# An attention whose opening is loaded through two queues, with the first head's rows ahead of the second's, fill-in products and new ranks

## The chip, the core and the metric

The kernel runs on one core of one Trainium2 chip. The metric is the device time of one execution in microseconds, as the median of several runs. A core has five instruction queues that matter here: TensorE (PE; its weight loads are listed as PEld), VectorE (DVE), ScalarE (ACT), GpSimd (POOL) and SyncE (SP), which only issues transfers (DMAs).

## The reference

The reference has two stages. The first is attention over 4 batches of 8 heads, with 768 rows of 64 numbers each. Queries and keys are each assigned to the nearest of 16 centroids, and a query sees only the keys of its own cluster:

```python
q_assign = np.argmax(np.einsum('bhsd,hcd->bhsc', q_n, c_n), axis=-1)
k_assign = np.argmax(np.einsum('bhsd,hcd->bhsc', k_n, c_n), axis=-1)
mask = q_assign[:, :, :, None] == k_assign[:, :, None, :]
scores = np.where(mask, scale * np.matmul(q, k.transpose(0, 1, 3, 2)), -1000000000.0)
attn = np.exp(scores - np.max(scores, axis=-1, keepdims=True))
attn = attn / (np.sum(attn, axis=-1, keepdims=True) + 1e-09)
x = np.matmul(attn, v)
```

The second stage is a mixture of experts on the 3072 x 512 result: gate weights that are balanced in eight rounds, and for each of 8 experts `h = relu(x @ w1[e])`, `out += P[:, e] * (h @ w2[e])`.

## The kernel before

**The units.** Heads are worked in pairs (two heads share the 128 partitions), and groups of four heads share the loads of v. For a pair the raw rows of q and k are transposed on PE (L636), copied (L646), and split in a high and a low part (`qH`, `kH` by a cast at L654 or L656, `qL`, `kL` by a subtraction at L658 on DVE or L660 on POOL), so that products keep f32 accuracy. `assign_pair` multiplies the transposed rows by the normed centroids (PE L685), transposes the result (L693) and finds for each row its cluster in a chain on DVE: maximum `mx` (L699), equality `ix` (L704 or L706), tie-breaking by the constants `rev` (L712), `mi` (L717), and a one-hot matrix (`tx` for the first pair at L723, `om` for later ones at L758). Transposed back (L732, L765), its rows go into `qX` and `kX` (for the first pair directly by ACT L746 and DVE L742; for later pairs over `ot`, L772, and DMAs). `place_pair` moves halves of `qH`, `kL` and so on to where the products want them, by DMAs (L790).

**The heads.** For each of 32 heads and 9 chunks of a 768 x 768 score matrix, PE makes masked maxima (`max_chunk`, L835) in one of two `max_ps` buffers and DVE reduces them (L839). `max_rows` turns the maxima into three rows of `qX` (a reduce at L858, ACT L860, POOL L862 and L863; for heads 0 and 1 PE L873 and ACT L878, for later heads PE L885, ACT L889 and DMAs L893, L903). Only then can `exp_chunk` make the scores (PE L923, L924) and ACT the exponentials `pe` (L930), which POOL sums (L945). `values` multiplies by v (PE L978, L986), and `norm` scales the result and makes the second stage's input. Parts of the second stage (weights read and scaled early, `scan_early` and others) fill gaps; the experts' products (L1356, L1540 to L1542, L1814) make up the rest of the time.

**The order.** Inside the attention the order of the instructions on each engine is fixed when the program is built. Each unit is a process that yields its next step as `(engine, cost)`, and the class `Planner` lists the steps by start time and rank. A rank is

```python
return n * NCH + c + KEYS[stage] - (KEYS["first"] if n == 0 and stage in FIRST else 0)
```

and among the steps that could start within `EARLY` (`PATIENCE` after the first 30 of the plan's own time units) of the first one on that engine, the lowest rank goes first. Where a step could run on one of two engines, `RELUCT` weighs the choice. The numbers in these tables have no direct meaning, they are picked. On the chip each engine then runs its list in order and waits where an operand is late.

**The opening before the change.** SP issues the centroids (L356), q and k of pair 0 (L554), v (L567), q of pair 1, the gate's weights `wg` (L224), and k of pair 1, in this order. PE transposes the normed centroids first (L377), then q and k.

## Time and profile before

| what | value |
|---|---|
| median of three runs | 2289.27 us (2289.05 to 2291.24) |
| the profiled execution | 2289.5 us, of which 2287.7 us are the profile's span |
| PE busy | 2257.7 us of the span, 99% |
| DVE, ACT, POOL busy | 1637.3, 1113.2 and 1145.9 us |

The span is the time from the first to the last instruction of the profile, and the 1.8 us beside it lie outside the profile. A busy share says only that an instruction of the engine was under way: PE busy for 99% of the span has 1% of it without any instruction, and where that 1% lies is what the rows below show.

### The profile page before, as it was taken

To read this page: it belongs to the slowest core of one execution; us is meant where nothing else is said; L and a number is where in the kernel's file an instruction comes from. 1 tells how busy PE (TensorE), PEld (TensorE's weight loads), DVE (VectorE), ACT (ScalarE), POOL (GpSimd) and SP (SyncE) were. 2 spreads that over 40 slices of the span, in tenths; PEclk is the share of its full clock that TensorE was granted. 3 is DMA by queue.
4 is the path that set the end of the run, shared out by engine and by line. 5 is a ranking of instruction groups with operands and counts; after the bars stand their busy time and mean duration, and the time that the engine had idled before them with its cause. 6 is when DMAs were issued, how large, how long until landed. Compare 5 with 4: busy or idle time off the path is not lost.

```text
span 2287.7 us, 39676 instructions
## 1 busy us (share of the span) xinstructions
PE 2257.7 (99%) x15491; PEld 1523.3 (67%) x15491; DVE 1637.3 (72%) x2691; ACT 1113.2 (49%) x2048; POOL 1145.9 (50%) x1009
## 2 busy tenths in 40 slices
PE   7999999999999999999999999999999999999998
PEld 4656665545555555567777777777777777777777
DVE  7767777648666776578888886776676666666667
ACT  5666676556666665344444443333434333333333
POOL 6676777865554555456566563333332323222233
PEclk9999999999999999999999999999999999999999
DMA  7556666446645643676666665544444554344433
GB/s 173 120 125 162 168 157 159 118 167 239 196 150 170 195 158 131 221 262 212 211 233 219 226 222 177 169 128 152 151 159 137 187 169 133 129 132 137 143 116 102
DMA packets 226828, 383.93 MB, mean 168 GB/s; under 512 B 73408, under 2 KB 154640, under 8 KB 226128
## 3 DMA queue, kind: packets, MB, share of 16 engines
q1 hardware_dynamic: 226208, 379.82, 52.6%
q8 instruction: 121, 1.98, 0.4%
q10 hardware_dynamic: 432, 1.57, 0.2%
q14 instruction: 67, 0.55, 0.1%
HBM read 272.22 MB, written 80.62 MB: 154 GB/s over the span
## 4 chain that ended last, share of the span: by engine, by line
PE 92%; DVE 3%; DMA 2%; ACT 1%; POOL 1%; issue 1%; SPq 0%; ACTq 0%; DVEq 0%; POOLq 0%
PE h_ps L1356 37%; PE pb L1814 12%; PE pc L1814 8%; PE pa L1814 8%; PE av_ps L978 5%; PE o_ps L1540 3%; PE o_ps L1542 3%; PE o_ps L1541 3%; PE max_ps L835 3%; PE exp_ps L923 3%; PE exp_ps L924 2%; PE misc_ps L636 1%; PE misc_ps L1020 1%; POOL psum L945 1%; DVE mrt L839 1%
## 5 line engine op out<-in xcount | busy, mean ns | idle before, releaser
L1356 PEld LDWEIGHTS <-wa 128*128 128x128 f16 x5376 | 525.7, 98 | 300.0 <-issue 2.1
L1814 PEld LDWEIGHTS <-ho 128*128 128x128 f16 x6048 | 591.4, 98 | 139.7 <-DVE ho L1708 2.5
L1356 PE MATMUL h_ps<-xsT,wa 128*128 128x384 f16 x3072 | 581.6, 326 | 0.3 <-DVE u L1370 0.2
L1699 POOL TENSOR_TENSOR B<-B,B 128x768 f32<-128x768 f32 x96 | 196.5, 2049 | 488.2 <-DVE ho L1708 468.0
L1356 PE MATMUL h_ps<-xsB,wa 128*128 128x384 f16 x2304 | 436.7, 326 | 0.3 <-ACT m L1379 0.3
L1708 DVE TENSOR_TENSOR ho<-B,ho 128x768 f16<-128x768 f32 x288 | 350.2, 1217 | 0.1
L1370 DVE SCALAR_TENSOR_TENSOR u<-h_ps,m 128x384 f32<-128x384 f32 x256 | 141.7, 554 | 271.1 <-PE h_ps L1356 267.0
L1854 ACT ACTIVATE B<-B 128x384 f32<-128x384 f32 x288 | 149.7, 520 | 378.8 <-DVE B L1370 375.4
L1814 PE MATMUL pb<-w2o,ho 128*128 128x256 f16 x2592 | 328.7, 273 | 0.4 <-DVE ho L1708 0.4
L1704 ACT CAST ho<-B 128x768 f16<-128x768 f32 x288 | 230.3, 825 | 11.2 <-POOL B L1699 7.8
L839 DVE TENSOR_REDUCE mrt<-max_ps 128x1 f32<-128x512 f32 (+1 forms) x288 | 190.5, 685 | 54.3 <-PE max_ps L835 52.7
L945 POOL TENSOR_TENSOR psum<-psum,pe 128x512 f32<-128x512 f32 x160 | 208.0, 1318 | 35.0 <-ACT pe L930 28.1
L1814 PE MATMUL pa<-w2o,ho 128*128 128x256 f16 x1728 | 219.2, 273 | 1.2 <-DVE ho L1708 1.2
L1814 PE MATMUL pc<-w2o,ho 128*128 128x256 f16 x1728 | 219.2, 273 | 0.2 <-DVE ho L1708 0.2
L1699 POOL TENSOR_TENSOR B<-B,T 128x768 f32<-128x768 f32 x48 | 94.6, 1973 | 230.0 <-DVE ho L1708 207.7
L930 ACT ACTIVATE pe<-exp_ps 128x512 f32<-128x512 f32 x288 | 166.9, 598 | 51.2 <-PE exp_ps L924 39.5
L1379 ACT ACTIVATE m<-h_ps 128x384 f32<-128x384 f32 x128 | 62.6, 489 | 191.0 <-PE h_ps L1356 187.2
L1852 ACT ACTIVATE B<-h_ps 128x384 f32<-128x384 f32 x96 | 47.1, 490 | 203.3 <-PE h_ps L1356 203.3
L1542 PE MATMUL o_ps<-wb,hl 128*128 128x512 f16 x384 | 145.5, 379 | 0.0
L1541 PE MATMUL o_ps<-wb,hh 128*128 128x512 f16 x384 | 145.5, 379 | 0.0
L1540 PE MATMUL o_ps<-wb,hh 128*128 128x512 f16 x384 | 145.5, 379 | 0.0
L1370 DVE SCALAR_TENSOR_TENSOR B<-h_ps,u 128x384 f32<-128x384 f32 x192 | 105.9, 552 | 48.3 <-PE h_ps L1356 48.2
(266 smaller groups left out, 3320.8 us busy)
## 6 DMA issues: line engine op xcount, KB each, us to landing
wa<-w1d SPq DMA_DIRECT2D x98, 896.0 KB
w2o<-w2d SPq DMA_DIRECT2D x168, 512.0 KB
raw<-in_moe_w SPq DMA_DIRECT2D x64, 512.0 KB
w1d<-wa SPq DMA_DIRECT2D x30, 896.0 KB
r<-in_moe_w SPq DMA_DIRECT2D x28, 512.0 KB
w2d<-w2s SPq DMA_DIRECT2D x28, 512.0 KB
w2d<-wb SPq DMA_DIRECT2D x96, 128.0 KB
scan<-in_moe_w SPq DMA_DIRECT2D x32, 256.0 KB
```

Of the source, the lines that this page charges most:

```text
L839: nc.vector.tensor_reduce(out=t["mr"][:, i0 : i0 + ni, ni - 1], in_=ps.rearrange("p (x c) -> p x c", x=ni), axis=AX, op=ALU.max)
L930: nc.scalar.activation(pe, ps.rearrange("p (x c) -> p x c", x=ni), AF.Exp, scale=SCALE)
L945: (nc.gpsimd if e == POOL else nc.vector).tensor_tensor(out=st[:, o : o + N0], in0=old[o], in1=part, op=ALU.add)
L1356: nc.tensor.matmul(ps[:, 0:HB], wa[:, w_, a, c, :], x[:, x_, c, :], start=(first and s_ == 0), stop=(s_ == len(steps) - 1), skip_group_che ...
L1370: nc.vector.scalar_tensor_tensor(out=t, in0=ps[:, 0:HB], scalar=KAPPA, in1=x, op0=ALU.mult, op1=ALU.add)
L1540: nc.tensor.matmul(po[i], hh[:, t, ti], wbh[:, t], start=(first and t == 0), stop=False)
L1541: nc.tensor.matmul(po[i], hh[:, t, ti], wbl[:, t], start=False, stop=False)
L1542: nc.tensor.matmul(po[i], hl[:, t, ti], wbh[:, t], start=False, stop=(last and t == 1))
L1699: nc.gpsimd.tensor_tensor(out=t, in0=d[a], in1=d[c], op=ALU.subtract)
L1704: nc.scalar.copy(t[:, 0], blocks[n, g][o])
L1708: nc.vector.tensor_tensor(out=t[:, 1], in0=blocks[n, g][o], in1=t[:, 0], op=ALU.subtract)
L1814: nc.tensor.matmul(ps[:, q], h[:, h_, f, q * P : (q + 1) * P], w[:, 2 * g + f, w_], start=(first and g == 0 and s_ == 0 and q % 2 == 0), s ...
```

## The change

The change touches the opening of the attention, and some things that go on through all heads.

- **Two queues.** `load_first` issues q of pair 0 on SP as the first transfer of all, with the centroids behind it, and k on ACT's queue. The norm of the centroids (`csq`, `cnorm`, `cs`) becomes part of the process `centroid_rows` and is planned. The gate's weights are loaded behind the rows of head 1 (`gate_weights`), and some small constants are made later or no longer.
- **First head ahead of the second.** `assign_first` runs the DVE chain of pair 0 in two halves, head 0 first. `first_rows` transposes each head's q and k columns apart: 24 transposes of 32 x 128 in place of 6 of 128 x 128. `split_first` separates raw copy, high part and low part into steps with their own ranks.
- **Maxima in two parts.** `first_max` makes head 0's rows for its first four row tiles once chunks 0 to 5 are reduced, and those of the last two after chunk 8. The exponentials of head 0 go in the order `ORDER0`.
- **Products of constants.** `fill` issues bf16 products 128 x 384 of the constant `rev` into an `av_ps` buffer that nothing reads: 7 ahead of everything, and others where the planner sees PE idle in the first 36 of its time units. There are 41.
- **Fewer transfers.** From head 2 on, the two maxima rows go into `qX` in one DMA instead of two, and the two flag rows into `nht` in one (`mm` gets a fourth block for it).
- **Ranks.** `KEYS`, `EARLY`, `PATIENCE` and `RELUCT` get other numbers; loads of weights count as landed 1.5 later (`SLACK`). Over the program ACT makes all high parts (18 casts of DVE go to ACT), and 12 of DVE's subtractions go to POOL.

The diff, cut to its core:

```diff
--- before.py
+++ after.py
-    EARLY = {'PE': 0.171, 'ACT': 0.241, 'DVE': 0.196}
-    PATIENCE = {'PE': 0.009, 'ACT': 0, 'POOL': 0.384, 'SP': 0.102, 'DVE': 0.013}
+    FILLED = 36.0
+    EARLY = {'PE': 0.05, 'ACT': 0.01, 'DVE': 0.27, 'POOL': 0.06}
+    PATIENCE = {'PE': 0, 'ACT': 0.05, 'POOL': 0.69, 'SP': 0.06, 'DVE': 0.0}
...
+            if engine == "PE" and start < self.FILLED:
+                self.fill(int((start - self.free["PE"] - 0.2) * (3.0 if start < 10.0 else 4.5)))
...
-    nc.sync.dma_start(out=wg[:, :, 0:E], in_=w_gate.rearrange("(c p) e -> p c e", p=P))
...
-        nc.sync.dma_start(out=cn, in_=centroids.rearrange("h c d -> (h c) d"))
...
+            yield ev["load", 0, "k", "begun"]
+            yield ACT, 1.5
+            nc.scalar.activation(begun, ones[:, 0:1], AF.Sqrt)
+            yield ev["cn"]
+            yield DVE, 0.45
+            nc.vector.tensor_tensor(out=csq, in0=cn, in1=cn, op=ALU.mult)
+            nc.vector.tensor_reduce(out=cnorm, in_=csq, axis=AX, op=ALU.add)
+            yield ACT, 0.2
+            nc.scalar.activation(root, cnorm, AF.Sqrt)
+            yield DVE, 0.6
+            nc.vector.tensor_scalar(out=cnorm, in0=root, scalar1=1e-6, scalar2=None, op0=ALU.add)
+            nc.vector.reciprocal(cnorm, cnorm)
+            for x in range(2):
+                nc.vector.tensor_scalar(out=cs[:, x, :], in0=cn, scalar1=cnorm, scalar2=None, op0=ALU.mult)
...
+        def gate_weights():
+            yield ev["rows", 1]
+            yield SP, 3.1
+            nc.sync.dma_start(out=wg[:, :, 0:E], in_=w_gate.rearrange("(c p) e -> p c e", p=P))
+            plan.copied(0.3)
...
-        mm = [sm.tile([P, 3 * NT], F32R, name=f"mm{i}", bufs=1) for i in range(3)]
+        mm = [sm.tile([P, 4 * NT], F32R, name=f"mm{i}", bufs=1) for i in range(3)]
...
+        filler = rev.rearrange("p t c g -> p (t c g)")
+
+        def fill(n):
+            if n > 0:
+                ps = ps_v.tile([P, 1024], F32, name="av_ps")
+                for _ in range(n):
+                    nc.tensor.matmul(ps[:, 0:384], filler[:, 0:P], filler, start=True, stop=True)
+
+        plan.fill = fill
+        fill(7)
+        plan.free.update({PE: 4.0, ACT: 0.7, DVE: 3.0, POOL: 3.0, SP: 0.7})
...
-        KEYS = dict(load=-86.738, split0=-192.873, split1=-34.701, split2=-32.207, assign=-24.965, place=-68.504, chain=-64.418, ones=-184.712, max=-12.015, rows=-187.596, exp=8.794, values=49.904, out=19.77, batch=-51.141, group=-31.02, vsum=-10.101, group0=-186.961, inputs=-298.614, first=1197.688)
...
+        KEYS = dict(load=-49.03, split0=-481.28, split1=-156.05, split2=-168.62, assign=-129.16, place=418.41, chain=-633.91, ones=120.85, max=54.78, rows=-75.5, exp=67.53, values=104.0, out=44.0, batch=91.92, group=-108.42, vsum=45.1, group0=-435.34, inputs=-608.95, first=1434.49, high=23.78, low=-357.87, chain1=-806.64, ones1=-49.74)
...
-        RELUCT = [6.752, 2.462, 2.782, 2.846, 0.115, 0.25, -0.214, 1.339, -1.014, -0.069, 0.985]
-
...
+            if p == 0:
+                for w in (("q", q, nc.sync, SP, 4.9), ("k", k, nc.scalar, ACT, 5.1)):
+                    plan.spawn(load_first(*w), plan.now.key)
+                return
...
+            yield SP, 1.62
...
+        def load_first(name, src, by, engine, landed):
+            yield engine, 0.76 if name == "k" else 1.2
+            a = pairs[0][name] = nat.tile([P, NT, 2, D], F32, name=f"{name}n")
+            by.dma_start(out=a, in_=src[0, 0:2].rearrange("h (p t) d -> p t h d", t=NT))
+            if name == "q":
+                nc.sync.dma_start(out=cn, in_=centroids.rearrange("h c d -> (h c) d"))
+                ev["cn"].set(plan, 4.0)
+            plan.queues = landed - 0.95
+            ev["load", 0, name].set(plan, landed)
+            ev["load", 0, name, "begun"].set(plan)
...
+                if p == 1:
+                    if w == todo[-1][0]:
+                        t_x.put(plan)
+                    yield POOL, 0.2 + (z - a) * 0.0019
+                    nc.gpsimd.tensor_tensor(out=lo, in0=raw(p, w)[:, a:z], in1=hi.bitcast(F32), op=ALU.subtract)
...
+            N = 2 * NT
+            ix = nat.tile([P, N // 2, C, 4], BF16, name="ix", bufs=1).rearrange("p t c g -> p (t c g)").rearrange("p (x n c) -> p x n c", x=2, c=C)
+            mx, mi = (nat.tile(shape, dt, name=nm, bufs=1) for nm, shape, dt in (("mx", [P, 2 * N], F32), ("mi", [P, N // 2, 4], BF16)))
+            mi = mi.rearrange("p t g -> p (t g)")
+            om = om0[:, 0 : S // 2].bitcast(BF16).rearrange("p (x n c) -> p x n c", x=2, n=N)
+            for x in range(2):
+                plan.now.key = urgency("chain" if x == 0 else "chain1", 0)
+                sc = ps2[:, 0 : 2 * N * C].rearrange("p (n x c) -> p x n c", x=2, c=C)[:, x]
+                m, l, i_ = mx[:, x * N : (x + 1) * N], mi[:, x * N : (x + 1) * N], ix[:, x]
+                wide = lambda t: t.unsqueeze(2).broadcast_to([P, N, C])
+                yield DVE, 0.65
+                nc.vector.tensor_reduce(out=m, in_=sc, axis=AX, op=ALU.max)
+                nc.vector.tensor_tensor(out=i_, in0=sc, in1=wide(m), op=ALU.is_equal)
+                yield DVE2, 0.9
+                nc.vector.tensor_tensor(out=i_, in0=i_, in1=rev0.unsqueeze(1).broadcast_to([P, N, C]), op=ALU.mult)
+                nc.vector.tensor_reduce(out=l, in_=i_, axis=AX, op=ALU.max)
+                nc.vector.tensor_tensor(out=om[:, x, :, 0:C], in0=i_, in1=wide(l), op=ALU.is_equal)
+                if x:
+                    t_s.put(plan)
+                for j in (1, 0):
+                    plan.spawn(first_rows(om, x, j), urgency("ones" if x == 0 else "ones1", 0))
...
+        def first_rows(om, x, j):
+            yield t_m
+            yield PE, 0.25, 0.053, 0.06
+            psb = ps_m.tile([P, 512], F32, name="max_ps").bitcast(BF16)
+            for i in range(NT):
+                a = i % 2 * HS + i // 2 * P
+                nc.tensor.transpose(out=psb[0:Q, a : a + P], in_=om[:, x, 2 * i + j], identity=ident_b)
+            yield ev["clear", 0]
+            e = yield (ACT, 0.72), (DVE, 0.89)
+            o = buffers(0)[f"{'qk'[j]}X{x}"][64 : 64 + C, :]
+            if e == DVE:
+                nc.vector.tensor_scalar(out=o, in0=psb[0:C, 0:S], scalar1=(1.0, BIG)[j], scalar2=(0.0, -BIG)[j], op0=ALU.mult, op1=ALU.add)
+            elif j:
+                nc.scalar.activation(o, psb[0:C, 0:S], AF.Identity, scale=BIG, bias=om_neg[0:C, :])
+            else:
+                nc.scalar.copy(o, psb[0:C, 0:S])
+            t_m.put(plan)
+            ev["x", 0, x, "qk"[j]].set(plan)
...
+        def first_max(n):
+            m_ = mm[n]
+            mr = sm.tile([P, NT], F32, name="mr1")
+            for part, (i0, i1, c0, c1) in enumerate(((0, 4, 0, 6), (4, 6, 6, 9)) if n == 0 else ((0, NT, 0, NCH),)):
+                for c in range(c0, c1):
+                    yield ev["m", n, c]
+                t = heads[n]
+                k_ = i1 - i0
+                yield DVE, 0.09
+                nc.vector.tensor_reduce(out=mr[:, i0:i1], in_=t["mr"][:, i0:i1], axis=AX, op=ALU.max)
+                m3 = m_.rearrange("p (j t) -> p j t", j=4)[:, :, i0:i1]
+                yield ACT, 0.19
+                nc.scalar.copy(m3[:, 0], mr[:, i0:i1])
+                yield POOL, 0.59
+                nc.gpsimd.tensor_scalar(out=m3[:, 2], in0=mr[:, i0:i1], scalar1=-BIG / 2, scalar2=None, op0=ALU.is_le)
+                nc.gpsimd.tensor_tensor(out=m3[:, 1], in0=mr[:, i0:i1], in1=m3[:, 0].bitcast(F32), op=ALU.subtract)
+                if i1 == NT:
+                    plan.spawn(flag(n, mr), plan.now.key + 1)
+                if n:
+                    yield ev["rows", 0]
+                yield PE, 0.08 + 0.06 * k_, 0.107, 0.06
+                ps = ps_v.tile([P, 1024], F32, name="av_ps")
+                for i in range(i0, i1):
+                    nc.tensor.transpose(
+                        out=ps.bitcast(F32R)[0:3, i * P : (i + 1) * P], in_=m_.rearrange("p (j t) -> p t j", j=4)[:, i, 0:3], identity=ident_r
+                    )
+                for a, z in SPANS:
+                    if i0 * P <= a < i1 * P:
+                        yield ACT, 0.15 + (z - a) * 0.00083
+                        nc.scalar.copy(t["qa"][96:99, a:z], ps[0:3, a:z])
+                ev["half", n, part].set(plan)
+            ev["rows", n].set(plan)
...
-                yield SP, 1.5
-                for j in range(2):
-                    nc.sync.dma_start(
-                        out=qa[96 + j : 97 + j, :].bitcast(F32).rearrange("o (t p) -> o t p", p=P), in_=mt[j * NT : (j + 1) * NT, :]
-                    )
...
+            nc.sync.dma_start(out=qa[96:98, :].bitcast(F32).rearrange("o (t p) -> o t p", p=P), in_=mt[0 : 2 * NT, :])
...
-            for j in range(n % 2 * 2, n % 2 * 2 + 2):
-                nc.sync.dma_start(out=nh[j : j + 1, :].bitcast(F32).rearrange("o (t p) -> o t p", p=P), in_=flagged)
...
+            for r in (slice(j, j + 2),) if n > 1 else (slice(j, j + 1), slice(j + 1, j + 2)):
+                nc.sync.dma_start(out=nhs[n // 2 % 3][r, :].bitcast(F32).rearrange("o (t p) -> o t p", p=P), in_=flagged)
...
+        ORDER0 = (0, 1, 3, 4, 6, 7, 2, 5, 8)
...
-            yield ev["rows", n]
+            yield ev["half", 0, 0] if n == 0 and c % 3 < 2 else ev["rows", n]
...
-                yield ev["begun", n, c - 1]
+                yield ev["begun", n, ORDER0[ORDER0.index(c) - 1] if n == 0 else c - 1]
...
+        SLACK = 1.5
...
+                    yield plan.copied(1.1) - plan.now.time + SLACK```

**In the order, first place: PE from the start to the first chain.** `qn`, `kn` are the raw rows, `cs` the normed centroids, `cm` their transposed form, `rev` the constant of the fill-in products. Before:

```order
L377 MATMUL misc_ps<-ident,cs 128x128
L636 MATMUL misc_ps<-ident,qn 128x128 x4
L636 MATMUL misc_ps<-ident,kn 128x128 x4
L636 MATMUL misc_ps<-ident,qn 128x128 x2
L636 MATMUL misc_ps<-ident,kn 128x128 x2
L685 MATMUL exp_ps<-qn,cm 32x384
```

In the changed kernel, behind nine fill-in products (their repeats are left out in the middle):

```order
L677 MATMUL misc_ps<-ident,qn 128x128 x6
L677 MATMUL misc_ps<-ident,kn 128x128 x2
L677 MATMUL max_ps<-ident,kn 128x128 x4
L510 LDWEIGHTS rev
L510 MATMUL av_ps<-rev 128x384
...
L378 MATMUL misc_ps<-ident,cs 128x128
L717 MATMUL misc_ps<-ident,qn 128x128 x4
L764 MATMUL exp_ps<-qn,cm 32x384
```

The transposes of pair 0 now stand first, then ten products of constants (one is shown), and the centroids' transpose, which stood ahead of all, behind them; four transposes of pair 1 stand between it and the assignment.

**Second place: ACT, from the rows of head 1 on.** `pe` are exponentials, `ot` the one-hot rows of a later pair, `qX_200` and `qX_225` hold head 1's rows, and `spread` is a constant. Before:

```order
L878 CAST qX_225<-av_ps 3x512
L878 CAST qX_225<-av_ps 3x256
L646 COPY qn<-misc_ps 128x256
L646 COPY kn<-misc_ps 128x256
L930 ACTIVATE pe<-exp_ps 128x512
L646 COPY qn<-misc_ps 128x512
L930 ACTIVATE pe<-exp_ps 128x512
L654 CAST qH_205<-misc_ps 128x512
L930 ACTIVATE pe<-exp_ps 128x512 x2
```

In the changed kernel:

```order
L1037 CAST qX_200<-av_ps 3x512
L733 CAST qH_182<-misc_ps 128x256
L1037 CAST qX_200<-av_ps 3x256
L922 ACTIVATE ot<-misc_ps,om_bias,om_scale 64x384
L733 CAST kH_198<-misc_ps 128x256
L1115 ACTIVATE pe<-exp_ps 128x512
L486 CAST spread<-three_682 36x768
L1115 ACTIVATE pe<-exp_ps 128x512
L724 COPY qn<-misc_ps 128x512
L1115 ACTIVATE pe<-exp_ps 128x512
L733 CAST qH_180<-misc_ps 128x512
L1115 ACTIVATE pe<-exp_ps 128x512 x2
```

Copies and high parts of the next pairs stand among the exponentials in both. `ot` and `spread`, which stood ahead of head 0's exponentials before, now stand among them too.

**Third place: PE, where a pair's maxima begin.** The numbers are those of buffers; `kX_231` before and `kX_206` in the changed kernel are those of the head whose maxima begin. Before, with the semaphores that are waited for:

```order
L835 MATMUL max_ps<-kX_231,qX_227 128x512 [waits DMAHW6_49,DMAHW5_49,DVE_49]
L835 MATMUL max_ps<-kX_231,qX_227 128x512 [waits DVE_49]
L923 MATMUL exp_ps<-qL_218,kH_222 128x512 [waits Activation_49]
L924 MATMUL exp_ps<-qX_226,kX_230 128x512
L923 MATMUL exp_ps<-qH_205,kL_208 128x256 [waits Activation_49]
L924 MATMUL exp_ps<-qX_211,kX_214 128x256
```

In the changed kernel:

```order
L992 MATMUL max_ps<-kX_190,qX_187 128x512 [waits DVE_49] x2
L992 MATMUL max_ps<-kX_190,qX_187 128x256 [waits DVE_49]
L992 MATMUL max_ps<-kX_190,qX_187 128x256
L992 MATMUL max_ps<-kX_206,qX_202 128x512 [waits DMAHW4_49,DMAHW7_49,DMAHW2_49,DVE_49]
L992 MATMUL max_ps<-kX_206,qX_202 128x512 [waits DVE_49]
L992 MATMUL max_ps<-kX_206,qX_202 128x256 [waits DVE_49]
L992 MATMUL max_ps<-kX_206,qX_202 128x256
```

Where two maxima stood between exponentials' products before, six chunks of maxima in a row now stand there, and each needs one of the two buffers that DVE's reduces set free.

## Rows read from the trace of the kernel before

**Rows 1.** The page: the chain that ended last, shares of the span by engine.

```profile
PE 92%; DVE 3%; DMA 2%; ACT 1%; POOL 1%; issue 1%; SPq 0%; ACTq 0%; DVEq 0%; POOLq 0%
```

**Rows 2.** Windows: busy us of each engine (PE, PEld, DVE, ACT, POOL), PEclk, DMA.

```profile
0.00:32.00 32.00, 20.30 (x79) 11.27 (x79) 21.81 (x67) 14.08 (x28) 20.54 (x47) 0.96 0.64 155
32.00:51.70 19.70, 18.59 (x104) 14.27 (x102) 17.02 (x29) 15.21 (x31) 13.35 (x13) 0.89 0.74 180
51.70:100.00 48.30, 48.11 (x300) 28.25 (x300) 37.10 (x69) 27.58 (x64) 31.87 (x39) 1.00 0.58 133
```

**Rows 3.** Timeline: SP's issues and PE's first transposes (start, us, engine, line).

```profile
1.18 0.76 SPq L554 DMA_DIRECT2D qn<-in_q  x1
1.98 0.84 SPq L554 DMA_DIRECT2D kn<-in_k  x1
5.08 1.12 PE L636 MATMUL misc_ps<-ident,qn 128*128 128x128 f32 x4 [0.24 <-DMA qn<-in_q]
5.21 3.83 SPq L224 DMA_DIRECT2D wg<-in_moe_w_gate  x1
6.96 1.09 PE L636 MATMUL misc_ps<-ident,kn 128*128 128x128 f32 x4 [0.76 <-DMA kn<-in_k]
```

**Rows 4.** Timeline: the first pair's chain on DVE and its rows.

```profile
13.13 0.56 DVE L699 TENSOR_REDUCE mx<-exp_ps 128x24 f32<-128x384 f32 x1 [1.46 <-PE exp_ps L693]
15.29 0.79 DVE L723 TENSOR_TENSOR tx<-ix,mi 128x384 bf16<-128x384 bf16 x1
16.14 0.82 PE L732 MATMUL exp_ps<-ident_b,tx 128*128 128x128 bf16 x6 [0.91 <-DVE tx L723]
17.05 0.79 ACT L746 CAST qX<-exp_ps 16x768 fp32r<-16x768 bf16 x1 [1.20 <-PE exp_ps L732]
17.94 0.95 DVE L742 TENSOR_SCALAR kX<-exp_ps 16x768 fp32r<-16x768 bf16 x1 [1.26 <-ACT qX L746]
```

**Rows 5.** Timeline: DVE's first reduces, and the second pair's chain.

```profile
20.87 0.69 DVE L839 TENSOR_REDUCE mrt<-max_ps 128x1 f32<-128x512 f32 x1
25.55 3.30 DVE L839 TENSOR_REDUCE mrt<-max_ps 128x1 f32<-128x512 f32 x5
29.12 0.54 DVE L699 TENSOR_REDUCE mx<-misc_ps 128x24 f32<-128x384 f32 x1
31.27 0.36 DVE L758 TENSOR_TENSOR om<-ix,mi 128x384 bf16<-128x384 bf16 x1
```

**Rows 6.** Timeline: rows and first exponentials of heads 0 and 1, first values.

```profile
29.85 0.81 PE L873 MATMUL av_ps<-ident_r,mm 128*3 128x128 f32 x6 [0.44 <-POOL mm L863]
30.48 0.83 ACT L878 CAST qX<-av_ps 3x512 fp32r<-3x512 f32 x2 [0.32 <-PE av_ps L873]
31.94 0.78 PE L923 MATMUL exp_ps<-qH,kL 128*128 128x512 f32 x1
43.56 0.48 PE L923 MATMUL exp_ps<-qL,kH 128*128 128x512 f32 x1
51.70 2.58 PE L978 MATMUL av_ps<-pe,vn 128*64 128x512 f32 x14
```

**Rows 7.** Lines by form, 0 to 110 us: busy us, mean ns of one | idle before.

```profile
L654 ACT CAST kH<-misc_ps 128x512 fp32r<-128x512 f32 x5 | 3.0, 598 | 0.0
L930 ACT ACTIVATE pe<-exp_ps 128x512 f32<-128x512 f32 x50 | 29.0, 599 | 11.4 <-PE exp_ps L924 6.5 <-PE av_ps L978 2.0 <-PE misc_ps L885 2.0
L772 ACT ACTIVATE ot<-misc_ps,om_bias,om_scale 64x384 f32<-64x384 bf16 x8 | 5.3, 668 | 5.6 <-PE misc_ps L765 5.6
L472 ACT CAST spread<-three 36x768 bf16<-36x768 f32 x1 | 0.8, 826 | 0.0
```

**Rows 8.** Windows and timeline: PE at its two rates.

```profile
32.00:34.00 2.00, 2.00 (x8) 1.67 (x7) 1.54 (x3) 1.74 (x3) 0.00 (x0) 0.50 0.02 3
34.00:36.00 2.00, 2.00 (x8) 1.65 (x8) 1.66 (x4) 1.09 (x2) 0.81 (x1) 0.50 0.93 211
39.28 0.60 PE L636 MATMUL misc_ps<-ident,qn 128*128 128x128 f32 x4
```

289 lines of the change are left out of this document (173 added, 116 removed).

## The prediction

> **What bounds the kernel now.** I began with the chain that ended last [rows 1]. PE holds 92% of it, and DVE, DMA, ACT and POOL share what is left, so time can be won only where PE stands still or runs slowly. The windows say where that is [rows 2]. From 51.7 us on, PE is busy for 48.11 of 48.30 us: from the first product with v (51.70 [rows 6]) there is so much independent work that it hardly waits. Ahead of it PE is busy for 20.30 + 18.59 = 38.9 of 51.7 us. So 12.8 us are empty, and part of the rest is slow: in 32 to 36 us the granted clock is 0.50, the lower level of 1.2 GHz [rows 8], and four transposes that take 0.60 us at 39.28 [rows 8] take 1.12 at 5.08 [rows 3], though the clock column reads 1.00 there. The change works in these 52 us.
>
> Within them a chain across engines decides. In the timeline q is awaited until 5.08 and k until 6.96 [rows 3]; the chain of pair 0 runs on DVE from 13.13 to 16.08, and the rows go over ACT and DVE to 18.89 [rows 4]; DVE reduces head 0's maxima from 20.87 to 28.85 [rows 5]; the rows are done at 31.31, and the first scores start at 31.94 [rows 6]. For head 1 they start at 43.56, and the values at 51.70 [rows 6]. Were these three points all earlier by the same time, the kernel would be shorter by it.
>
> **The change part by part.** The sum is made against the profiled execution, 2289.5 us, which is 0.2 above the median.
>
> *Loads.* Before, q is issued at 1.18 and k at 1.98 [rows 3]. Now both start at about 0.7, so both end their issue near 1.5, where k ended it at 2.82 before. Bounds for the landing are 4.6 (q earlier by what it is issued earlier) and 7.0 (k as before); I take 5.4 for both, a third of the way, since k's issue is now where q's was. A rule speaks against this part. What the rows show: k is issued 0.80 us behind q, but its transposes start 1.88 us behind q's [rows 3]; something other than the issue spreads them. The Trainium skill, DMA: Bandwidth & Descriptors, Issuing engines are not separate DMA queues, says that transfers from several engines run on the same 16 DMA engines and interleave, and that only the issuing time is saved. By that, k gains about its issue and q loses what k takes of the bandwidth; by that alone k would land 1.3 earlier than before (the end of its issue, 2.82 to 1.5), at 5.7, and the sum would change by 0.3.
>
> *Centroids.* They land behind q now, and their norm, transpose and copies stand between q, k and the assignment on three engines. I count 2 us from q and k to the copies' end and 1.1 for the assignment, then `tr` and its transposes. From landed k to the chain took 6.2 us before (6.96 to 13.13), and I leave it 7.1: the chain starts near 12.5, 0.6 earlier. Bounds are 11.5 and 13.5: ten fill-in products stand ahead of the centroids' transpose on PE and could run on when it is ready.
>
> *Half a chain first.* The chain took 2.95 us for both heads [rows 4]. Half of its columns need less, but not half, since five operations start: I take 1.9, to 14.4. Then half of the transposes' 0.82 (I take 0.5), and `kX` and `qX` made side by side by ACT and DVE where they were made one behind the other (0.79, then 0.95 after a wait of 1.26 [rows 4]): head 0's maxima start near 16.1. The second half of the chain (1.07) then goes ahead of the first reduce, which I put at 17.1. It was at 20.87: **3.8 us** earlier. The 24 small transposes cost PE about 1 us more than six (18 x 0.06), in time that is empty.
>
> *Maxima in two parts.* Six reduces at 0.65 (five in 3.30 [rows 5]) end 4.0 behind the first. From the last reduce to the rows' end took 2.46 (28.85 to 31.31); with four tiles instead of six, half of the copies, and a few fill-in products I take 2.2. So head 0's first scores stand near 23.3, **8.6 us** earlier than 31.94. For head 1, 18 reduces (11.7) and the second pair's chain (31.63 - 29.12 = 2.5 [rows 5]) lie on DVE, then the rows (2.5), and about 1.6 for what else stands between: 18.3 behind the first reduce, near 35.4. That is **8.2 us** earlier than 43.56; the subtractions that went from DVE to POOL are in it.
>
> *From head 1's scores to the values.* Here the gain is at risk. In the order ACT has, between the first rows of head 1 and the next pairs' maxima, six full conversions at 0.60, five exponentials at 0.60, two `ot` at 0.67, `spread` at 0.83 [rows 7], the rows' copies of 0.83 [rows 6] and seven smaller ones, some 11.6 us. Before, `ot` and `spread` were behind it by then. DVE's subtractions and maxima wait for these casts. If all this stands in line, the values begin at 35 us behind the first reduce, 52.1, where they began at 51.70, and nothing is won. If the work that now comes earlier fills the time, the whole 8.2 is won, less 0.4 for work that PE has more of ahead of the values (four more transposes, one more vsum product, the 1 us of small transposes, two maxima fewer). I have no row that decides between these ends. I take half: **-4.1 us**.
>
> *Fill-in products.* They write a buffer that nobody reads, and stand where PE would be empty. At nothing, as long as the next operand is late; ten of them at the lower rate would hold the centroids' transpose for 1 to 2 us if it is ready early, which is in the bounds above. What they do to the clock is a rival.
>
> *Transfers, weights of the gate, SLACK.* 60 DMAs fewer leave SP's queue. All DMA waits together are 2% of the chain [rows 1], and no row says how much of it is theirs: bounds -3 and 0, and I take 0, for the rows of a later head have a head's time ahead of them. `wg` held SP for 3.83 us ahead of k of pair 1 [rows 3]; moved, it holds the moves of later pairs, at most 3.8 us for these alone, hidden behind the pair that is under way. SLACK delays early weights for which PE does not wait here: 0.
>
> *Casts and subtractions.* ACT takes 18 casts of DVE, about 8 us at 0.60 or less each [rows 7] over all heads. ACT is busy for 27.58 of 48.30 us [rows 2], so I cost it at nothing; without that cover it is at most 8.
>
> Sum: 2289.5 - 4.1 = **2285.4 us**.
>
> **The rivals.** *The clock stays up.* The granted clock fell before, after a stretch in which PE waited for DVE between maxima, and was 0.50 through 32 to 36 us [rows 8] in which PE had work all along. If the fill-in products hold it at 2.4 GHz, head 0's scores also run at twice the rate, some 2 to 4 us more, and nothing goes back: -8 to -13. For it: several of the products stand exactly ahead of head 0's scores, where the clock was low. Against it: they stand in gaps of a plan, and real gaps may lie elsewhere. The Trainium skill, TensorE: Matmul & The Clock Gate, Part 1, says that activity releases the throttle, which is for this rival; its Part 4 says that transposes do not count the same way, and most of the opening's early work is transposes. The trace agrees in so far as the first transposes ran at half rate [rows 3]. Chance 0.20.
>
> *The opening moves and the end does not.* The values start where they started, for the queue of ACT above, and what was done early only leaves other gaps: -2 to +3, chance 0.15.
>
> *Slower: maxima in bursts.* PE fills one of two `max_ps` buffers while DVE reduces the other, so two reduces (1.3 us) must pass between a chunk and the one after the next. Where PE has less other work between them in its list, it waits. By the durations of the rows, counted along the order, 9 such places lacked 2.3 us in all before, and 34 lack 13.7 now. If DVE is not ahead there, up to 11.4 us come back over all heads, and with part of the opening's gain kept the kernel is 4.6 to 10 slower. Against it: DVE is busy for 37.1 of 48.3 us [rows 2], and where PE comes late to a burst nothing is lost. It decides when more than some 8 of the 11.4 us are real. Chance 0.15.
>
> **How the numbers follow.** The likeliest case, part of the gain kept, has 0.50 and its own range from 2281.3 (all of 8.2) to 2290. A change of 0.2%, 4.6 us, is what a measurement of this kernel can tell from none. Of the 0.50, 0.24 lie below -4.6 and 0.26 above. Faster: 0.24 + 0.20 = 0.44. Same: 0.26 + 0.15 = 0.41. Slower: 0.15. For the range I go 11.5 down, which leaves out the far end of the clock's case, and 4.5 up, which leaves out most of the bursts': 2278 to 2294.
>
> **What would show it.** In the trace after: k's first transposes below 6; the first reduce near 17, head 0's first scores near 23 and head 1's near 35 (each right or wrong by itself); the values' first product between 43.5 and 52 (my sum says 47.6); the granted clock from 20 to 36 us (near 1 is the first rival's case); idle time of PE put down to `mrt` behind 52 us (over 8 us is the third's). The prediction is wrong if the values start as late as before, if the fill-in products turn the clock, or if the gain of the opening is paid back by waits for maxima.

## The result, and the profile after

The changed kernel takes 2307.67 us (median of six runs, 2306.82 to 2308.81) against 2288.91 us before: the ratio is 1.0082 with a 95% interval from 1.0069 to 1.0095. It is 18.8 us slower, where 2285.4 was forecast.

The first view is the windows of the changed kernel (columns as in [rows 2]).

```profile
0.00:52.00 52.00, 42.97 (x209) 26.70 (x210) 30.22 (x77) 27.25 (x55) 38.71 (x67) 0.85 0.66 146
52.00:66.00 14.00, 7.91 (x37) 4.58 (x37) 8.62 (x18) 3.86 (x10) 8.58 (x14) 0.74 0.71 170
66.00:110.00 44.00, 43.62 (x271) 24.88 (x270) 26.03 (x49) 23.55 (x54) 27.07 (x33) 0.98 0.36 82
```

PE is full from 66 us on, where it was full from 52 us on [rows 2]. The 42.97 us of the first row hold 11.8 us of fill-in products (the windows of L510 alone). Without them PE has been busy by 66 us for as long as it had been by 52 before (39.1 and 38.9 us).

The timeline of the changed kernel shows what came when (start, us, engine, line). L591 are the loads, L677 the transposes of q, L374 and L378 the centroids, L764 and L837 the assignments of the first and the second pair, L785 the start of the first chain, L996 DVE's reduces, L806 the transposed one-hot rows, L1108 scores, L992 maxima, L630 the sums of v, L1163 the values and L1545 the experts.

```profile
0.72 0.71 ACTq L591 DMA_DIRECT2D kn<-in_k  x1
0.72 0.77 SPq L591 DMA_DIRECT2D qn<-in_q  x1
7.31 1.51 PE L677 MATMUL misc_ps<-ident,qn 128*128 128x128 f32 x6 [2.05 <-DMA qn<-in_q]
11.12 1.17 DVE L374 TENSOR_SCALAR cs<-cn,cnorm 128x64 f32<-128x64 f32 x2
12.91 0.27 PE L378 MATMUL misc_ps<-ident,cs 128*128 128x128 f32 x1
13.73 0.51 PE L764 MATMUL exp_ps<-qn,cm 128*32 128x384 f32 x1
15.80 0.36 DVE L785 TENSOR_REDUCE mx<-exp_ps 128x12 f32<-128x192 f32 x1 [2.12 <-PE exp_ps L773]
21.02 2.56 DVE L996 TENSOR_REDUCE mrt<-max_ps 128x1 f32<-128x512 f32 x4
28.31 0.82 PE L806 MATMUL max_ps<-ident_b,tx 128*32 128x128 bf16 x6
30.16 0.88 PE L1108 MATMUL exp_ps<-qH,kL 128*128 128x512 f32 x1
31.40 0.85 PE L837 MATMUL misc_ps<-qn,cm 128*32 128x384 f32 x1
33.53 1.29 DVE L996 TENSOR_REDUCE mrt<-max_ps 128x1 f32<-128x512 f32 x2 [1.99 <-PE max_ps L992]
42.92 0.47 PE L1108 MATMUL exp_ps<-qL,kH 128*128 128x512 f32 x1
53.97 0.69 PE L992 MATMUL max_ps<-kX,qX 96*128 96x512 f32 x2
63.78 0.79 PE L630 MATMUL misc_ps<-vsum,ones 128*128 128x256 f32 x1 [4.66 <-POOL vsum L626]
65.78 3.54 PE L1163 MATMUL av_ps<-pe,vn 128*64 128x512 f32 x16
509.97 1.14 PE L1545 MATMUL h_ps<-xsB,wa 128*128 128x384 f16 x6
```

The kernel before has the second pair's assignment and the first product of the experts here:

```profile
22.34 0.85 PE L685 MATMUL misc_ps<-qn,cm 128*32 128x384 f32 x1
491.72 1.14 PE L1356 MATMUL h_ps<-xsB,wa 128*128 128x384 f16 x6
```

Read against [rows 3 to 6]: q's transposes start 2.2 us later than before, the first reduce at the same time (21.02 and 20.87), head 0's scores 1.8 us earlier, head 1's 0.6 us earlier, and the values 14.1 us later. The expert products begin at 509.97, before at 491.72: 18.2 us later, and what follows takes the same 1796 us. So the whole loss lies in the attention: 14.1 us by the first product with v, and some 4 us behind it.

For these 4 us one row stands out: PE's weight loads of the maxima from 75 us to the experts, by line, with the idle time ahead of them and what ended it. First the kernel before, then the changed one:

```profile
L835 PEld LDWEIGHTS max_ps<-kX,qX 96*128 96x128 f32 x327 | 56.2, 190 | 23.2 <-DVE mrt L839 7.6 <-DMA qX<-ot 2.8 <-issue 2.8
```

```profile
L992 PEld LDWEIGHTS max_ps<-kX,qX 96*128 96x128 f32 x342 | 59.2, 190 | 22.4 <-DVE mrt L996 12.5 <-issue 1.2 <-DMA kX<-ot 0.5
```

They waited 12.5 us for DVE's reduces, where they had waited 7.6. A weight load can wait while an earlier product still runs, so this is no measure of lost time by itself: between the first product with v and the experts PE is busy for 434.83 us in place of 430.20, with as many products (2680 and 2683), and without an instruction for 9.4 in place of 9.8 us. So the 4 us lie within PE's busy time, and the row alone doesn't show how many of them are the waits.

### The profile page after: what moved, and what is told of

Same layout as the page of the kernel before. It is cut to its first block, busy times and chain, and to the rows that moved or that the text cites. A ratio compares the mean times of both kernels' runs of the same rounds, so it can differ in the third digit from the quotient of the medians.

```text
span 2305.5 us, 39696 instructions
## 1 busy us (share of the span) xinstructions
PE 2273.9 (99%) x15550; PEld 1530.8 (66%) x15550; DVE 1626.2 (71%) x2676; ACT 1120.3 (49%) x2065; POOL 1156.8 (50%) x1021
## 4 chain that ended last, share of the span: by engine, by line
PE 92%; DVE 3%; POOL 1%; ACT 1%; issue 1%; DMA 0%; ACTq 0%; SPq 0%; DVEq 0%; POOLq 0%
PE h_ps L1545 37%; PE pb L2003 12%; PE pc L2003 8%; PE pa L2003 8%; PE av_ps L1163 5%; PE o_ps L1729 3%; PE o_ps L1730 3%; PE o_ps L1731 3%; PE exp_ps L1108 3%; PE max_ps L992 3%; PE exp_ps L1109 2%; DVE mrt L996 1%; PE misc_ps L1205 1%; PE misc_ps L717 1%; POOL psum L1130 1%
## 5 line engine op out<-in xcount | busy, mean ns | idle before, releaser
L1545 PEld LDWEIGHTS <-wa 128*128 128x128 f16 x5376 | 525.7, 98 | 299.6 <-issue 1.6
L1545 PE MATMUL h_ps<-xsT,wa 128*128 128x384 f16 x3072 | 581.6, 326 | 0.1
L1545 PE MATMUL h_ps<-xsB,wa 128*128 128x384 f16 x2304 | 436.7, 326 | 0.3 <-ACT m L1568 0.3
L996 DVE TENSOR_REDUCE mrt<-max_ps 128x1 f32<-128x512 f32 (+1 forms) x288 | 191.4, 686 | 68.1 <-PE max_ps L992 65.5
L1115 ACT ACTIVATE pe<-exp_ps 128x512 f32<-128x512 f32 x288 | 167.7, 600 | 53.9 <-PE exp_ps L1109 46.4
```

Source lines behind the costliest of these rows:

```text
L996: nc.vector.tensor_reduce(out=t["mr"][:, i0 : i0 + ni, ni - 1], in_=ps.rearrange("p (x c) -> p x c", x=ni), axis=AX, op=ALU.max)
L1115: nc.scalar.activation(pe, ps.rearrange("p (x c) -> p x c", x=ni), AF.Exp, scale=SCALE)
L1545: nc.tensor.matmul(ps[:, 0:HB], wa[:, w_, a, c, :], x[:, x_, c, :], start=(first and s_ == 0), stop=(s_ == len(steps) - 1), skip_group_che ...
```

## The experiments

Three theories on the opening stood first: **L**, two loads at once make q late; **F**, the fill-in products are in the way; **V**, the values wait in PE's list behind work that is late. The first four kernels tell them apart.

**e1, one queue.**

```diff
-                for w in (("q", q, nc.sync, SP, 4.9), ("k", k, nc.scalar, ACT, 5.1)):
+                for w in (("q", q, nc.sync, SP, 4.9), ("k", k, nc.sync, ACT, 5.1)):
```

> The changed kernel with k of pair 0 issued on SP behind q and the centroids; nothing else moves in any order. Theory L (the two loads share the DMA engines, so q lands at 7.3 us where it landed at 5.0 before, and the opening starts from there): q's first transpose near 5.5 instead of 7.3, the first reduce near 19.5 instead of 21.0, and the kernel 1 to 2 us faster than the changed one. Theory V (the time is lost in the order between head 1's scores and the first product with v): values still begin near 64 to 66 us, and the kernel is within 2 us of the changed one, near 2307.

2307.71 us, as the changed kernel. The timeline of e1 has q's transposes where L wants them:

```profile
5.33 1.17 PE L677 MATMUL misc_ps<-ident,qn 128*128 128x128 f32 x6
6.98 0.44 PE L677 MATMUL misc_ps<-ident,kn 128*128 128x128 f32 x2 [0.48 <-DMA kn<-in_k]
```

But the assignment starts at 13.17 (13.73 before the edit), since the centroids and the second pair's q stand ahead of it, the first reduce at 21.28, where L wanted 19.5, and the values at 65.69. L is right about q's landing, and by itself it changes nothing.

**e2, no fill-in products.**

```diff
-            if n > 0:
+            if n > 99:
                 ps = ps_v.tile([P, 1024], F32, name="av_ps")
```

> The changed kernel without its 41 products of constants (leaves out work that nothing reads). Theory F (the fill-in products hold up the centroids' transpose and heads' scores): the first reduce 1 to 2 us earlier and the kernel 1 to 3 us faster than the changed one. Rival (they keep the clock up and pay for themselves): the granted clock is lower between 12 and 24 us and the kernel 1 to 3 us slower. Theory V: within 1 us, values still near 65.

2309.56 us; the interval of its ratio to before, 1.0072 to 1.0099, overlaps that of the changed kernel. The first reduce starts at 20.82 and the values at 64.82, so F falls. Its rival is not settled: the granted clock from 12 to 24 us is 0.68 in place of 0.96, as the rival has it, but the 1.9 us of time can't be told from none.

**e3, the first group's sums ranked lower.**

```diff
-            plan.now.key = urgency("vsum", n)
+            plan.now.key = urgency("vsum", n) - (200.0 if n == 0 else 0.0)
```

> The changed kernel with the rank of the sums of v of the first group of heads lowered by 200, so that on PE their product (L630) stands ahead of head 1's scores' end and the first product with v stands ahead of the second group's. Theory V (the first product with v waits in PE's list behind the second group's product, for which POOL's ten additions were awaited for 4.7 us): values begin near 57 to 59 instead of 65.8, and the kernel is 6 to 9 us faster than the changed one, near 2300. Theory L or F: values' start moves but other waits take its place, and the kernel stays within 2 us of 2307.

2302.34 us, 5.3 less. The product of the sums and the first product with v in the timeline of e3:

```profile
49.53 1.05 PE L630 MATMUL misc_ps<-vsum,ones 128*128 128x256 f32 x2
54.84 1.51 PE L1163 MATMUL av_ps<-pe,vn 128*64 128x512 f32 x6
```

In the changed kernel these sums stood at 57.87, and the values behind the second group's product, for whose sums PE waited 4.66 us (63.78 in the timeline). Now the values start 11 us earlier, more than V had, and half of that reaches the end: 5.3 us, a little below its range.

**e4, the kernel before with k on ACT's queue.**

```diff
-                nc.sync.dma_start(out=a, in_=src[b, 2 * hp_ : 2 * hp_ + 2].rearrange("h (p t) d -> p t h d", t=NT))
+                (nc.scalar if p == 0 and name == "k" else nc.sync).dma_start(out=a, in_=src[b, 2 * hp_ : 2 * hp_ + 2].rearrange("h (p t) d -> p t h d", t=NT))
```

> The kernel before, with k of pair 0 issued on ACT's queue and nothing else changed. Theory L: q and k land together near 6.5 to 7, k's wait goes and q's comes, and the kernel is 0 to 2 us slower than before. My forecast's step (q and k both land near 5.4): the chain of pair 0 starts about 1 us earlier and the kernel is up to 1 us faster. Theory V: nothing that can be measured.

2290.07 us, ratio 1.0001 (0.9993 to 1.0010): nothing that can be told. In its timeline q's transposes start at 6.32 instead of 5.08 [rows 3] and the values at 52.49 instead of 51.70 [rows 6], the way L has it and against my forecast's step.

What was left was why the second pair is late: its assignment starts at 31.40 in the changed kernel, at 22.34 before. `assign_pair` takes a token that the first pair gives back. Now that the second head's rows come last, the first pair holds it until they are written. That is theory **P** (the pair); theory **C** is the centroids' chain.

**e5, centroids first**, their norm ahead of the planned steps, and all three loads on SP (e1's edit too).

```diff
+        nc.sync.dma_start(out=cn, in_=centroids.rearrange("h c d -> (h c) d"))
         csq = nat.tile([P, D], F32, name="csq", bufs=1)
...
+        nc.vector.tensor_tensor(out=csq, in0=cn, in1=cn, op=ALU.mult)
+        nc.vector.tensor_reduce(out=cnorm, in_=csq, axis=AX, op=ALU.add)
...
         def centroid_rows():
-            yield ev["cn"]
-            yield DVE, 0.45
-            nc.vector.tensor_tensor(out=csq, in0=cn, in1=cn, op=ALU.mult)
...
```

> The changed kernel with the centroids as the first transfer, their norm ahead of the planned steps and all on SP's queue, as before; its planner moves other steps a little. Theory C (the centroids' norm behind q's copies on DVE holds pair 0's assignment until 13.7 us): assignment near 10, first reduce near 17.5 to 18.5 instead of 21.0, head 0's scores near 26 to 27, kernel 2 to 4 us faster than the changed one. Theory P (the second pair comes too late, whose assignment starts at 31.4 instead of 22.3): head 2's maxima and the values stay near 50 to 64, and the kernel is less than 2 us faster.

2311.67 us, 4 us slower where C had 2 to 4 faster. The assignment starts at 9.67, head 0's scores at 25.47 and the values at 53.76, all as C has them or better. The re-planned order has more bursts of maxima, chunks of maxima in a row that wait for DVE (16.4 us in the row of the weight loads instead of 12.5). These 3.9 us are not enough for 12 us of lost gain. The windows of e5 show more:

```profile
75.00:85.00 10.00, 8.30 (x42) 5.09 (x41) 9.29 (x18) 6.20 (x15) 8.99 (x12) 0.98 0.56 128
85.00:95.00 10.00, 9.42 (x32) 5.47 (x31) 7.33 (x14) 2.43 (x7) 3.71 (x8) 0.50 0.40 95
95.00:105.00 10.00, 9.26 (x25) 6.36 (x26) 7.71 (x15) 3.56 (x8) 2.06 (x5) 0.50 0.60 132
```

The granted clock is 0.50 from 85 to 105 us, behind a run of maxima that waited for DVE; in the changed kernel it is 1.00 there.

**e6, the token given back when the chain is done.**

```diff
+            t_sc.put(plan)
             for w in "kq":
                 yield ev["x", 0, 1, w]
             ev["om", 0].set(plan)
-            t_sc.put(plan)
```

> The changed kernel with one line moved: the token that lets the next pair's assignment begin is given back when the first pair's chain is done, not when the second head's rows of the first pair are written. Theory P: the second pair's assignment starts near 21 to 23 instead of 31.4, its first maxima near 46 to 49 instead of 54.0, and the kernel is 4 to 8 us faster than the changed one. Theory V alone (group 0's sums): the first product with v is still behind POOL's sums, and the kernel is within 2 us of 2307.

2305.24 us. The second pair's assignment starts at 20.52 and its maxima at 43.64 instead of 53.97, as P says. The values still wait for the sums, until 61.10, and 2.4 us reach the end, where P had 4 to 8.

**e7, e3 and e6 together; e8, with e5 too.**

> Both: the token given back early and the rank of the first group's sums lowered by 200. If P and V are two causes that add: 9 to 13 us faster than the changed kernel, 2295 to 2298. If they are one (PE lacks work in the same time): 5 to 7 us, as the group's rank alone, near 2301.

> Centroids ahead on SP, the token given back early, and the first group's rank lowered. If C, P and V are the opening's whole loss: 13 to 18 us faster than the changed kernel, 2290 to 2294, and what is left above the kernel before is the bursts of maxima (about 4 us in the trace of the changed kernel). If the opening has another cause: above 2297.

e7 takes 2306.64 us, slower than either expectation, although its values start at 52.36; e8 takes 2293.98, with values at 46.05. So P and V together are shown to be 13.4 of the 14.1 us by which the values were late, and an early opening alone doesn't decide the time. Behind its values e7 needs 456.82 us up to the experts, the changed kernel 444.19; its row of weight loads says 15.6 us, and its granted clock is 0.77 in 105 to 120 us and 0.66 in 320 to 330. Theory **B**, the bursts, was left to test. By the order alone I counted the places where two chunks of maxima have less than 1.25 us of other PE work between them, and what they lack: 2.4 us before, 13.8 in the changed kernel, 18.0 in e7, 10.8 in e8 (the last two counted after these kernels had run). One rank changes it.

**e9 and e10, the changed kernel with the rank of the maxima 30 or 70.**

```diff
-        KEYS = dict(... max=54.78, ...)
+        KEYS = dict(... max=30, ...)
```

> The changed kernel with the rank of the maxima 30 instead of 54.78; by the order the places where PE lacks work between two maxima fall from 34 to 12, and what they lack from 13.8 to 2.2 us. Theory B (bursts of maxima cost about 4 us behind the opening): the mean of a maxima product, start to next start behind 75 us, falls from 236 to about 224 ns as in the kernel before, and the kernel is 3 to 5 us faster than the changed one, near 2303. Rival (a burst costs nothing because PE is late to it): within 1 us of 2307.

> The changed kernel with the rank of the maxima 70 instead of 54.78: 88 places that lack 45.5 us in all, instead of 34 and 13.8. Theory B: the mean of a maxima product rises to 270 ns or more and the kernel is 8 to 20 us slower than the changed one, 2315 to 2327. Rival: within 3 us of 2307.

e9 takes 2311.71 us, e10 2345.57. The row of the weight loads, first of e9 and then of e10:

```profile
L992 PEld LDWEIGHTS max_ps<-kX,qX 96*128 96x128 f32 x344 | 56.8, 190 | 21.9 <-DVE mrt L996 6.6 <-issue 2.4 <-DVE mr L1054 2.2
```

```profile
L992 PEld LDWEIGHTS max_ps<-kX,qX 96*128 96x128 f32 x340 | 65.3, 211 | 42.4 <-DVE mrt L996 33.8 <-DVE kL L742 1.2 <-issue 1.1
```

e10 shows the mechanism beyond its range: 21 us more of waits, 38 us more of time (8 to 20 were expected). e9's waits fall by 6 us as expected, and the kernel is 4 us slower all the same. Its last heads are the reason that shows: behind 400 us PE waits 4.8 us for POOL's sums of the last heads and 3.3 for exponentials, 1.0 and 0.9 in the changed kernel, and in 505 to 515 us, where PE is busy for 4.88 of 10 us, the granted clock is 0.72. For e9 the total was forecast wrong.

**e11 and e12, e8 with the rank `max` 40, and with `exp` 64 beside it.**

> The kernel of e8 (centroids ahead, token early, first group's rank lowered; 26 places that lack 10.8 us) with the rank of the maxima 40: 8 places that lack 2.3 us. If what e8 leaves above the kernel before is the bursts: 3 to 5 us faster than e8, 2289 to 2291. If it is something else: within 1 us of 2294.

> As e11, with the rank of the exponentials 64 instead of 67.53: 4 places that lack 1.2 us. By theory B the same as e11 within 1 us; a difference beyond 2 us between the two would show that what a small move of ranks does to the rest of the order is as large as the effects looked for here.

2296.78 us and 2289.74 us (ratio to before 1.0001, 0.9992 to 1.0010). e12 has all of the loss back. e11 is no faster than e8, where B had 3 to 5 us, though its row of weight loads falls from 9.4 to 6.6 us; and with about as few bursts as e12 (6.2 us in the row) it is 7 us slower. So the rest of the order weighs as much as the bursts do.

**e13, the kernel before with its maxima rows moved by one DMA.**

```diff
-                for j in range(2):
-                    nc.sync.dma_start(
-                        out=qa[96 + j : 97 + j, :].bitcast(F32).rearrange("o (t p) -> o t p", p=P), in_=mt[j * NT : (j + 1) * NT, :]
-                    )
+                nc.sync.dma_start(out=qa[96:98, :].bitcast(F32).rearrange("o (t p) -> o t p", p=P), in_=mt[0 : 2 * NT, :])
```

> The kernel before with the two rows of maxima moved into qX by one DMA instead of two for 30 heads; no order changes but SP's. My forecast's term (nothing, bounds -3 and 0): within 1 us of the kernel before. Rival (SP's queue is on the path): 2 to 3 us faster.

2287.88 us, ratio 0.9994 (0.9985 to 1.0002): no difference that can be told, as forecast.

**e14, the kernel before with the rank `max` -2 instead of -12.015.**

> The kernel before with the rank of the maxima -2 instead of -12.015: 35 places that lack 12.4 us in all, instead of 9 and 2.4, nearly as many as in the changed kernel (34 and 13.8). Theory B: the mean of a maxima product behind 75 us rises from 224 to 233 to 240 ns and the kernel is 3 to 6 us slower than before, 2292 to 2295. Rival (the changed kernel's 4 us behind the opening come from the casts on ACT or the additions on POOL): within 1 us of before.

2299.36 us, 1.0042 (1.0029 to 1.0055), though its values start at 46.15, earlier than before. Its row:

```profile
L835 PEld LDWEIGHTS max_ps<-kX,qX 96*128 96x128 f32 x327 | 56.2, 190 | 23.1 <-DVE mrt L839 12.3 <-issue 4.0 <-PE max_ps L835 0.8
```

The wait is that of the changed kernel, 12.5, in a kernel without the change. So casts and additions on other engines aren't needed for it. The time exceeds the range; e14 also shows 1.4 us of waits for `qX`'s rows (0.2 before) and others that weren't there, so not all 10 us are the bursts'.

**e15, e6 with `max` 30; e17, e7 with `max` 40.**

> The kernel of e6 (token given back early) with the rank of the maxima 30: 11 places that lack 2.2 us, instead of 36 and 14.5. If the late second pair is most of the opening's loss and the bursts the rest: 2292 to 2297. If it is only one of three causes of like size: 2299 to 2303. Above 2303 the theory of the second pair falls.

> The changed kernel with the token given back early, the first group's rank lowered and the rank of the maxima 40 (10 places that lack 2.1 us); loads and centroids as in the change. If order and bursts are the whole loss and the loads cost nothing further: 2289 to 2292, as e12. If the loads and the centroids behind q cost what head 0's scores lose by them (3 to 4 us): 2293 to 2296. Above 2298 another cause is left.

2303.41 and 2294.49 us. With the bursts gone the second pair alone isn't enough (its values start at 61.17, behind the sums), and e15 lies at the limit of 2303 above which P was to fall. Pair and group together bring the values to 50.99 and win 13.2 us of the 18.8; e17 differs from e7 by the rank `max` and is 12.2 us faster. What is left to e12 is 4.8 us. Against the expectation of e17 this is not the loads and the centroids: e11 is e17 with these two changed, and it is no faster (2296.78 us). Only together with the rank `exp` 64 (e12) do the 4.8 us come, and what the loads and the centroids cost stays open.

**e16, e12 without fill-in products.**

> The kernel of e12 (as fast as the kernel before) without its products of constants; no order changes otherwise. If they hold the clock up in the opening, as the forecast's first rival had it: the granted clock falls between 20 and 36 us and the kernel is 2 to 4 us slower than e12. If they are worth nothing: within 1 us.

2290.44 us: the same as e12, as the second case has it. But the clock fell, as the first case has it. Windows 24 to 32 us, first of e12 and then of e16:

```profile
24.00:28.00 4.00, 3.14 (x29) 2.20 (x27) 3.72 (x17) 3.05 (x6) 3.07 (x7) 1.00 1.03 236
28.00:32.00 4.00, 3.84 (x20) 2.31 (x17) 3.93 (x8) 3.90 (x8) 3.24 (x6) 1.00 0.13 32
```

```profile
24.00:28.00 4.00, 3.98 (x18) 2.53 (x17) 3.73 (x17) 2.94 (x5) 2.79 (x7) 0.50 0.95 208
28.00:32.00 4.00, 3.93 (x17) 2.56 (x16) 2.32 (x5) 3.02 (x6) 2.58 (x4) 0.73 0.02 3
```

Without the products the granted clock is at its lower level, 1.2 GHz, from 24 to 28 us. Head 1's scores then start at 44.45 instead of 42.50 and the values at 53.01 instead of 51.09, but the experts at 491.41 and 492.23: the 2 us are made up behind. In 55 to 65 us it is e12 whose clock is lower, 0.83 against 1.00.

**e18, e12 with the second head's rows of the first pair ranked at -900.**

> The kernel of e12 with the rank of the second head's rows of the first pair lowered to -900, so that they are made ahead of head 0's last maxima. My forecast's step (head 1's maxima follow head 0's on DVE without a hole): head 1's scores near 37 to 39 instead of 42.5, and the kernel 1 to 4 us faster than before, if PE has work for it; more places that lack cover (14 and 3.2 us instead of 4 and 1.2) take up to 1 us of it. Rival (ACT and POOL are full there): head 1's scores stay above 41, and the kernel is within 2 us of 2289.

Head 1's scores start at 38.92 instead of 42.50, as forecast, but the kernel takes 2302.04 us, 13.5 more than before, where 1 to 4 less were expected: the values start at 57.28, 6 us later than in e12. A step was moved forward, and the list behind it came out worse.

## Why the prediction was wrong

**Loads.** Put at 5.4 with bounds 4.6 and 7.0; q took until 7.31, outside. Issue was not what q waited for: it is issued at 0.72 in e1 too, with k behind it on one queue, and is transposed from 5.33 on. In e4 the second queue alone moves q from 5.08 to 6.32. The Trainium skill, DMA: Bandwidth & Descriptors, Issuing engines are not separate DMA queues, says that transfers from several engines interleave and only the time to issue them is saved; the runs agree, and I had set it against this part without following it.

**Centroids.** The chain was put at 12.5 (at most 13.5) and started at 15.80. The late q is 2 us of it. Of the rest, most is DVE's list: the norm's second half stands behind the copies of q and k, and its last step takes 1.17 us for two instructions (11.12). About 1 us goes with the fill-in products: without them the assignment starts at 12.77 in place of 13.73 (e2).

**Half a chain first.** Right in its length: 5.2 us from chain to first reduce, where I had 4.6. The 3.8 us of gain became nothing, 3.3 through the two steps above and 0.6 here.

**Maxima in two parts.** 6.2 us from first reduce to head 0's scores became 9.1: the second head's transposes stand ahead of the scores on PE (28.31), and the granted clock was at its lower level, 0.50 for 24 to 32 us in the windows of the changed kernel:

```profile
24.00:28.00 4.00, 3.82 (x17) 2.27 (x17) 3.32 (x6) 0.23 (x2) 2.82 (x6) 0.50 0.16 35
28.00:32.00 4.00, 3.64 (x19) 1.86 (x20) 2.09 (x11) 2.11 (x4) 1.46 (x5) 0.50 0.01 2
```

So the rival of the clock fell too: with five fill-in products between 25.8 and 30.6 the clock was low all the same.

**Head 1.** I put 18 reduces on DVE in one line. They have a hole from 27.84, where head 0's last reduce ends, to 33.53: the second head's q rows are transposed only at 28.31, and head 0's first scores and the second pair's assignment stand behind them on PE. It took 21.9 us instead of 18.3.

**From head 1's scores to the values: the step that failed.** I bounded it by "nothing is won" (52.1) and "all of it" (43.5), as if the lists could only lose what they had gained. The 35 us behind the 52.1 are no sum of the terms I gave either: 18.3 and 11.6 make 29.9. The stretch took 22.9 us against 8.1 before, and the values began at 65.78. Two edits of the diff that I had passed over did it, and neither shows as a cost of an instruction: the first pair's token, which is given back only behind the second head's rows (P), and the first group's sums, which have a later rank (V). With both undone the values begin at 52.36 (e7). The sums also wait for `ev["rows", 0]` where they waited for `ev["om", 0]`; that wait stayed in every kernel here and is not tested apart. With the bursts taken out as well, 13.2 us are won (e17), and all of it with the centroids, the loads and the rank of the exponentials (e12), of which the loads and centroids by themselves win nothing (e11 against e17). How the 18.8 us split between P, V and B stays open, since each edit re-plans the whole order: e7 undid P and V and gained 1 us.

**Bursts.** The rival with a chance of 0.15 came nearest in time, and its mechanism is there, but not as the main loss: in the changed kernel at most the 4 us behind the values are the bursts', and the opening's gain that it kept was a loss. By its own sign, over 8 us of PE's idle time put down to `mrt` behind 52 us, it does not hold: PE's own rows have 2.8 us there (0.3 before), and the 12.5 are those of the weight loads. Its size was taken from the order at up to 11.4 us; the row of waits moved by 4.9 us. Over the kernels this row follows the count: 2.4 lacking give 7.6 us, 13.8 give 12.5, 18.0 (e7) give 15.6, 45.5 (e10) give 33.8. The time doesn't follow it: a lower rank `max` takes waits out each time, and e17 is 12.2 us faster than e7, e15 and e11 can't be told from e6 and e8, and e9 is 4.0 us slower than the changed kernel.

**Fill-in products, transfers.** At nothing, and no difference that can be told was measured for the products (e2, e16) and for the merged rows of maxima (e13). The other terms at nothing (the flag rows, the gate's weights, `SLACK`, the casts) were not tested apart.

No kernel tried here beats the kernel before: e12, e13 and e16 can't be told from it.

## What to carry to other kernels

- Where a planner's list runs on queues in order, look for what a step waits for by name (tokens, events, buffers) before pricing its instructions; a step that is moved behind another takes everything that its token holds with it.
- An early start is worth only what the next full engine gets of it: write down the time of the first instruction from which the bound engine never waits, and let the forecast be about that one, with a bound on the side of a loss.
- A count on the order (here: work between two uses of a pair of buffers) told which kernels would wait more, from e9 on before they ran, but not their total time; a rank that moves one step moves the rest by several us either way.

## What the runs showed of the hardware

The granted clock can fall in the middle of the attention with PE busy nearly all along. Windows of e10:

```profile
140.00:150.00 10.00, 8.80 (x42) 5.73 (x40) 8.61 (x15) 7.36 (x21) 8.00 (x13) 1.00 0.50 123
150.00:160.00 10.00, 9.43 (x32) 5.71 (x32) 7.31 (x14) 3.06 (x9) 4.58 (x7) 0.51 0.24 66
160.00:170.00 10.00, 9.35 (x32) 6.60 (x32) 7.77 (x16) 4.77 (x12) 2.05 (x5) 0.50 0.75 167
```

The fall comes behind maxima that wait for DVE (from 146 us on), and the clock stays low through the next 20 us. The falls in e5 (85 us) and e7 (110 and 321 us) also come behind such a run; that the run causes them is not shown apart. What they cost is an estimate from windows of 2 us between the first product with v and the experts, PE's busy time times what the granted clock lacks of 1: 27 us in e10, 16 in e5, 7 in e7, 3 in e9, 1 in the changed kernel, none in the kernel before. In e5, e7 and e10 this is more than the waits of the weight loads grew by.

A DVE instruction of 36 x 12 elements took 0.15 us before (at 28.77) and 0.96 and 1.19 us in the changed kernel (at 43.92 and 44.91), and each ended within 0.03 us of the end of one of POOL's additions (44.85 and 46.08). The Trainium skill, SBUF — State Buffer, "SBUF: two separate sides", says that DVE and GpSimd share a pair of ports, and that of a DVE instruction with two SBUF inputs and a GpSimd instruction that reads SBUF the first to start holds it to its end; the trace agrees. `spread` on ACT waited for them, between head 1's exponentials.
